# Moving the limit of the row-wise units and the time of eight early output projections in a fused attention and MLP kernel

## The chip, the cores and the metric

One core of one Trainium2 chip runs the whole program. The metric is the device time of one execution in microseconds (us). A single run differs from the next by 0.1 to 0.3%, so medians of several runs are compared, and where less than one per cent matters, both kernels run in turn on the same chip. The "span" of a run, from its first to its last instruction, is 1.7 to 2.3 us shorter than its time.

## The reference, cut to what matters

```python
# x: 2048 tokens x 512; 32 query heads, 8 KV heads, 2048 keys of 128 each
mod = silu(c) @ w_mod                       # six rows: sa, ca, ga, sb, cb, gb
h = layernorm(x) * (1 + ca) + sa
q = h @ wq
p = softmax(q k^T / sqrt(128));  o = p v    # the loop of 128 units
x = x + ga * (o @ wo)                       # the "output projections" of the units
h = layernorm(x) * (1 + cb) + sb            # second norm
z = gelu(h @ w_in); z1, z2 = halves of z    # z2 and z1 stages
g = w_sp @ layernorm(z2) + b_sp             # the "spatial product"
x = x + gb * ((z1 * g) @ w_out)
```

## The kernel before

A unit is one KV group (4 heads) with one tile of 128 queries. There are 128 units, and the main loop does one per iteration, in eight slots. "By columns" the scores come out with keys on the partitions, and PV is 64 small matmuls in the next iteration. "By rows" they come out with queries on the partitions; the rows are normalised by DVE (the vector engine) and turned by a transposing DMA, and PV is 16 wide matmuls three iterations later. An output projection, four matmuls, follows PV by two or three iterations.

```python
NU = HKV * NT                                   # 128;  CT = 4, NSLOT = 8
TURN_A, TURN_B = 2 * CT, NU - CT - 2            # 8, 122

def by_rows(u):  return TURN_A <= u < TURN_B and u % 2 == 0
def pv_at(u):    return u + 3 if by_rows(u) else u + 1
def wo_at(u):    return pv_at(u) + (3 if TURN_A <= u < TURN_B else 2)
# ... qk(u, i), rows branch: two matmuls, then
            nc.scalar.activation(out=rows_of(u, hh)[...], in_=s_ps[:], func=ACT.Exp,
                                 scale=inv_sqrt_dh, accum_out=rsums[u][:, i : i + 1])   # L1012
            if half == 1:
                at(*divmod(u * NSLOT + i + 2, NSLOT), lambda: turn_rows(u, hh))
# ... pv(u, i), by columns, after its last slot
            nc.sync.dma_start_transpose(out=oTs[u][:], in_=onorms[u]...)                # L1100
# ... wo_proj(u): four matmuls oT x wo (L1112); for the last group also residual and statistics
# ... ln2(it, j), the second norm of tile j
        def second():
            # ...
            normalise(xn[:], x_sb[:, j, :], ...)                                        # L686
            st["xnT"] = res.tile([P, NDT, P], BF16, name="xnT2", bufs=2)                # two buffers
            nc.sync.dma_start_transpose(out=st["xnT"][:], in_=xn[:])                    # L1149
        def third():
            # four tensor_scalar: hT <- xnT * (1 + cb) + sb                             # L1156
        at(it + 1, 0, first); at(it + 1, 4, second); at(it + 2, 5, third)
# ... loads
    at(2, 5, lambda: nc.gpsimd.dma_start(out=wmod_b, in_=wmod_dram[...]))               # 2 MB
    at(NU - CT - 1, 2, lambda: nc.gpsimd.dma_start(out=win_sb, in_=win_dram))
    at(4, 4, mod_cols_b)                        # first use of wmod_b: L855
    at(5, 4, mod_rows)
    # from iteration NU + 1 on: transposed loads of w_sp from SP                        # L1188
# ... main loop
    for it in range(NU + 6):
        pvs = [u for u in (it - 5, it - 3, it - 1) if 0 <= u < NU and pv_at(u) == it]
        wos = [u for u in range(max(it - 6, 0), min(it - 2, NU)) if wo_at(u) == it]
        wf = [fn for u in wos for fn in wo_proj(u)]
        for i in range(NSLOT):
            for fn in later.pop((it, i), []): fn()
            if it < NU: qk(it, i)
            # PV of pvs, this slot's part; then the fills (q projections)
            if i >= NSLOT - len(wf): wf[i - NSLOT + len(wf)]()
            if it >= NU: zrun(3)                # z2 and z1 matmuls
        # ... ln2(it, tile) for the units of the last group in wos
```

## Time and profile before

| | before |
|---|---|
| time of three runs, us | 1314.62, 1315.22, 1316.67; median 1315.22 |
| profiled run: time, span, granted clock | 1314.0, 1311.9, 1.0 |
| iteration 8, the first with scores by rows, starts at | 83.16 |
| iteration 120 starts at | 1056.22 |
| first z2, first z1, first spatial matmul | 1128.79, 1152.72, 1182.94 |
| first MLP output projection (L1458) | 1210.57 |

The table holds start times of TensorE from the timeline of its instructions; they cut the span into stretches that can be compared between kernels. In a timeline line the columns are start, duration of the group, engine, source line, operation, output<-inputs, shapes, count, and in brackets the idle time ahead of it with what ended it. Matmuls overlap, so the price of a group is the distance to the next start, not its duration. The lines themselves stand in the prediction below.

### The profile page before, as it was taken

The numbers are of one execution on the slowest core, as the hardware profiler recorded it, in microseconds if no ns is written. First come the engines' busy times: TensorE is split into PE (matmuls) and PEld (weight loads), VectorE is DVE, ScalarE is ACT, GpSimd is POOL, SyncE is SP. The second block draws the span as 40 slices with busy tenths as digits, with TensorE's granted clock in tenths as the row PEclk, the third lists the DMA queues.
The fourth block names the chain that finished last, engine by engine and source line by source line (L and its number), as shares of the span: only waits on it lengthen the run. The fifth ranks groups of instructions, "written<-read, shape, count | busy, mean of one in ns | idle before, by whom it ended". The sixth has DMA issues, their size and how long they took to land.

```text
span 1311.9 us, 24470 instructions
## 1 busy us (share of the span) xinstructions
PE 1304.1 (99%) x9623; PEld 741.0 (56%) x9623; DVE 682.6 (52%) x1675; ACT 1111.1 (85%) x1517; POOL 54.0 (4%) x96
## 2 busy tenths in 40 slices
PE   9999999999999999999999999999999999999998
PEld 5665555555555555555555555555555556644445
DVE  5644544444445454444545444444454577884444
ACT  7899999999999999999999999999999998650000
POOL 1200000000000000000000000000000011120000
PEclk9999999999999999999999999999999999999999
DMA  7589778977787797779986798678866673254300
GB/s 181 119 118 178 130 140 147 148 130 149 153 156 142 140 140 142 142 139 136 160 162 121 144 142 156 124 150 153 153 125 128 116 131 85 58 138 100 73 20 27
DMA packets 592170, 170.51 MB, mean 130 GB/s; under 512 B 581712, under 2 KB 588112, under 8 KB 592048
## 3 DMA queue, kind: packets, MB, share of 16 engines
q1 hardware_dynamic: 585024, 149.74, 64.5%
q0 software_dynamic: 4432, 16.91, 5.1%
q10 hardware_dynamic: 2592, 2.23, 0.5%
q8 instruction: 77, 1.26, 0.4%
q14 instruction: 45, 0.37, 0.1%
HBM read 21.89 MB, written 2.10 MB: 18 GB/s over the span
## 4 chain that ended last, share of the span: by engine, by line
PE 98%; DMA 1%; DVE 0%; ACT 0%; SPq 0%; issue 0%; DVEq 0%
PE o_ps L1080 19%; PE s_ps L1024 18%; PE s_ps L1005 15%; PE o_ps L1059 15%; PE misc L1112 8%; PE misc L945 8%; PE misc L1437 7%; PE s_ps L1271 2%; PE s_ps L1310 2%; PE o_ps L1458 1%; DMA oT<-onorm 1%; PE o_ps L786 1%; PE s_ps L1458 1%; PE misc L855 0%; PE o_ps L945 0%; DVE hT L814 0%
## 5 line engine op out<-in xcount | busy, mean ns | idle before, releaser
L1031 ACT ACTIVATE pT<-s_ps 128x1024 bf16<-128x1024 f32 x560 | 568.5, 1024 | 34.4 <-PE s_ps L1024 11.3
L1080 PEld LDWEIGHTS <-pT 128*128 128x128 bf16 x4480 | 299.6, 98 | 130.8
L1080 PE MATMUL o_ps<-v,pT 128*128 128x129 bf16 x4480 | 344.6, 220 | 0.0
L1024 PE MATMUL s_ps<-qT,kT 128*128 128x512 bf16 x1136 | 337.6, 379 | 0.3 <-ACT pT L1031 0.2
L1005 PE MATMUL s_ps<-kT,qT 128*128 128x512 bf16 x912 | 271.2, 379 | 0.0
L1012 ACT ACTIVATE win_sb<-s_ps 128x1024 bf16<-128x1024 f32 x228 | 233.3, 1024 | 3.4
L1112 PE MATMUL misc<-wo_g,oT 128*128 128x512 bf16 x512 | 194.1, 379 | 0.7 <-DMA oT<-onorm 0.7
L945 PE MATMUL misc<-hT,wq_g 128*128 128x512 bf16 (+2 forms) x520 | 187.0, 371 | 0.1
L1024 PEld LDWEIGHTS <-kT 128*128 128x128 bf16 x1136 | 110.2, 98 | 114.6 <-issue 2.4
L1012 ACT ACTIVATE pn<-s_ps 128x1024 bf16<-128x1024 f32 x152 | 155.4, 1023 | 2.0 <-ACT wmod_a L1012 0.3
L1059 PEld LDWEIGHTS <-v 128*128 128x128 bf16 x912 | 89.2, 98 | 107.7
L956 DVE CAST qT<-misc 128x512 bf16<-128x512 f32 x125 | 85.6, 684 | 123.1 <-PE misc L945 123.1
L1068 DVE CAST oT<-o_ps 128x512 bf16<-128x512 f32 x57 | 39.4, 691 | 192.3 <-PE o_ps L1059 192.3
L1059 PE MATMUL o_ps<-wsp,v 128*128 128x512 bf16 x464 | 137.3, 379 | 0.0
L1059 PE MATMUL o_ps<-pT,v 128*128 128x512 bf16 x448 | 133.2, 379 | 0.0
L1005 PEld LDWEIGHTS <-qT 128*128 128x128 bf16 x912 | 89.1, 98 | 59.8 <-issue 0.2
L1045 DVE TENSOR_TENSOR tot<-rs 128x1 f32<-128x1 f32 x228 | 35.0, 153 | 127.7 <-ACT win_sb L1012 85.3
L1437 PE MATMUL misc<-wsp,z 128*128 128x512 bf16 (+2 forms) x560 | 100.7, 336 | 0.0
L1050 DVE TENSOR_SCALAR win_sb<-win_sb,rall 128x2048 bf16<-128x2048 bf16 x114 | 85.9, 753 | 4.2 <-DVE rall L1048 0.3
L1437 PEld LDWEIGHTS <-z 128*128 128x128 bf16 x560 | 50.6, 98 | 48.5
L1012 ACT ACTIVATE wmod_a<-s_ps 128x1024 bf16<-128x1024 f32 x76 | 77.8, 1024 | 0.0
L1125 DVE TENSOR_TENSOR xacc<-misc,xacc 128x512 f32<-128x512 f32 x112 | 76.1, 679 | 0.0
(110 smaller groups left out, 831.0 us busy)
## 6 DMA issues: line engine op xcount, KB each, us to landing
wq_g<-in_A_wq_dram POOLq DMA_DIRECT2D x7, 512.0 KB, 6.1
v<-in_A_v_cache_dram POOLq DMA_DIRECT2D x7, 512.0 KB, 6.3
wo_g<-in_A_wo_dram POOLq DMA_DIRECT2D x7, 512.0 KB, 10.6
wsp<-in_w_mod_dram POOLq DMA_DIRECT2D x1, 2048.0 KB, 10.8
out_dram<-yout ACTq DMA_DIRECT2D x16, 128.0 KB, 1.7
win_sb<-in_B_w_in_dram POOLq DMA_DIRECT2D x1, 1792.0 KB, 7.9
x_sb<-in_A_x_dram SPq DMA_DIRECT2D x3, 512.0 KB, 5.9
oT<-onorm SPq DMA_TRANSPOSE x71, 2.8
```

Of the source, the lines that this page charges most:

```text
L945: nc.tensor.matmul(ps[0][:, o0 : o0 + n], lhsT=wqs[g][:, dt, hh * DH : (hh + 1) * DH], rhs=hTs[ch][:, dt, c0 : c0 + n], start=(dt == 0), s ...
L956: nc.vector.tensor_copy(out=dst, in_=src)
L1005: nc.tensor.matmul(s_ps[:, c * 512 : (c + 1) * 512], lhsT=qTs[b][:, hh, jj * P : (jj + 1) * P], rhs=groups[g]["kT"][:, k0 : k0 + 512], sta ...
L1012: nc.scalar.activation(out=rows_of(u, hh)[:, half * HK : (half + 1) * HK], in_=s_ps[:], func=ACT.Exp, scale=inv_sqrt_dh, accum_out=rsums[u ...
L1024: nc.tensor.matmul(s_ps[:, h * 512 : (h + 1) * 512].rearrange("p (r q) -> p r q", r=REP), lhsT=groups[g]["kT"][:, kt * P : (kt + 1) * P], ...
L1031: nc.scalar.activation(out=pTs[u][:, 2 * i : 2 * i + 2, :], in_=s_ps[:].rearrange("p (k q) -> p k q", k=2), func=ACT.Exp, scale=inv_sqrt_dh,)
L1050: nc.vector.tensor_scalar(out=rows, in0=rows, scalar1=rinv, scalar2=None, op0=ALU.mult)
L1059: nc.tensor.matmul(o_pss[u][:], lhsT=groups[g]["v1"][:, kt, 0:DH], rhs=pTs[u][:, kt, :], start=(kt == 0), stop=(kt == NKT - 1),)
L1080: nc.tensor.matmul(o_ps[:, hh % 2, 0 : DH + 1], lhsT=pTs[u][:, kt, hh * P : (hh + 1) * P], rhs=groups[g]["v1"][:, kt, 0 : DH + 1], start=( ...
L1112: nc.tensor.matmul(X_ps[:], lhsT=oTs[u][:, hh, :], rhs=groups[g]["wo"][:, hh, :], start=(hh == 0), stop=(hh == REP - 1),)
L1125: nc.vector.tensor_tensor(out=xaccs[j][:], in0=X_ps[:], in1=xaccs[j][:], op=ALU.add)
L1437: nc.tensor.matmul(g_ps[:, :n], lhsT=z2[:, st, f * P : (f + 1) * P], rhs=wsp[t][:, st, c0 : c0 + n], start=(st == 0), stop=(st == NT - 1 a ...
```

## The change

The intent has two parts. **Part one** turns units 122 and 124 from columns to rows, and so the load of `win_sb`, which overwrites row buffers, has to be issued later. **Part two** puts the output projections of units 0 to 7 three iterations behind PV instead of two, as the later units have it. The last units, which come after unit 121, are two iterations behind.

```diff
-    TURN_A, TURN_B = 2 * CT, NU - CT - 2
+    TURN_A, TURN_B = 2 * CT, NU - 2
@@
-        return pv_at(u) + (3 if TURN_A <= u < TURN_B else 2)
+        return pv_at(u) + (3 if u < TURN_B - CT else 2)
@@
-    at(NU - CT - 1, 2, lambda: nc.gpsimd.dma_start(out=win_sb, in_=win_dram))
+    at(NU - 2, 4, lambda: nc.gpsimd.dma_start(out=win_sb, in_=win_dram))
```

## The prediction

> **What bounds the kernel now.** The page first: share of busy time per engine, then the slices.
>
> ```profile
> PE 1304.1 (99%) x9623; PEld 741.0 (56%) x9623; DVE 682.6 (52%) x1675; ACT 1111.1 (85%) x1517; POOL 54.0 (4%) x96
> ```
>
> TensorE is busy 99% of 1311.9 us. That count may hide pipelining, so I read its spacing in the timeline of its instructions. The attention loop runs one unit (four heads of 128 queries against 2048 keys) per iteration, in eight slots. A unit is done either "by columns" (scores QK at L1024, PV at L1080: 64 small matmuls) or "by rows" (QK at L1005, PV at L1059: 16 wide ones, after a transposing DMA, three iterations later). One slot of each kind, from the regular part of the loop:
>
> ```profile
> 1056.22 0.59 PE L1005 MATMUL s_ps<-kT,qT 128*128 128x512 bf16 x2
> 1056.65 0.62 PE L1080 MATMUL o_ps<-v,pT 128*128 128x129 bf16 x8
> 1057.11 0.38 PE L945 MATMUL misc<-hT,wq_g 128*128 128x512 bf16 x1
> 1057.32 0.59 PE L1005 MATMUL s_ps<-kT,qT 128*128 128x512 bf16 x2
> ...
> 1065.03 0.59 PE L1024 MATMUL s_ps<-qT,kT 128*128 128x512 bf16 x2
> 1065.46 0.59 PE L1059 MATMUL o_ps<-pT,v 128*128 128x512 bf16 x2
> 1065.89 0.38 PE L945 MATMUL misc<-hT,wq_g 128*128 128x512 bf16 x1
> 1066.11 0.59 PE L1024 MATMUL s_ps<-qT,kT 128*128 128x512 bf16 x2
> ```
>
> The starts tell the price: two wide matmuls take 0.43 us (1065.46 to 1065.89), so **0.216 us** each; eight small ones take 0.455 us (1056.65 to 1057.11), so **0.057 us** each. A slot is 1.10 us with PV by columns, 1.08 by rows. No waits stand between them: here TensorE is the bound, at full clock (PEclk is 9 in every slice).
>
> ScalarE is the second limit. The timeline of its instructions gives one exp per 0.915 us where nothing holds it (1095.42: eight in 7.86 less start-up), but about 1.10 by rows, because a read of the accumulator follows each:
>
> ```profile
> 1056.86 1.02 ACT L1012 ACTIVATE win_sb<-s_ps 128x1024 bf16<-128x1024 f32 x1
> 1057.78 0.19 ACT L1012 ACTIVATION_READ_ACCUMULATOR win_sb<-s_ps 128x1 f32 x1
> 1057.95 1.02 ACT L1012 ACTIVATE win_sb<-s_ps 128x1024 bf16<-128x1024 f32 x1
> ```
>
> Where a unit's QK is by rows and a slot has no fill (no q projection L945, no output projection L1112), TensorE could do 0.43 + 0.455 = 0.885 us but is held at 1.00, as iteration 10 shows:
>
> ```profile
> 100.34 0.59 PE L1005 MATMUL s_ps<-kT,qT 128*128 128x512 bf16 x2
> 100.77 0.61 PE L1080 MATMUL o_ps<-v,pT 128*128 128x129 bf16 x8
> 101.34 0.59 PE L1005 MATMUL s_ps<-kT,qT 128*128 128x512 bf16 x2
> ```
>
> Last, the list of waits. The only sizable one of TensorE on another engine in the loop is this, and the chain of waits shows its source:
>
> ```profile
> 79.63 0.39 PE L1112 MATMUL misc<-wo_g,oT 128*128 128x512 bf16 x1 [0.72 <-DMA oT<-onorm]
> ```
>
> ```profile
> 66.82 12.77 DMA oT<-onorm
> ```
>
> **What the Trainium skill says.** "TensorE: Matmul & The Clock Gate", Back-to-back issue gap: the gap of an isolated warm matmul is N/2.4 + 2.5 ns, that is 216 ns at 512 columns and 56 at 129, but in streams of weight loads and matmuls about 131 and (at 128) 81. This trace has 0.216 and 0.057 although every matmul here has its own weight load, so it agrees with the isolated formula, not the stream figures. This matters: at 81 ns a unit by columns would cost 64 x 0.081 = 5.2 us and the change would gain over 1.5 us per unit. "Perfetto Trace Analysis", Identifying the Most-Contended Engine: matmul busy share does not tell how near the roofline TensorE is. Agreed; hence the spacing above. "DMA: Bandwidth & Descriptors", Issuing engines are not separate DMA queues: DMAs from all engines share the 16 DMA engines and interleave. The trace agrees: the oT transpose above took 12.8 us (median 2.8) behind four hT transposes, with three loads of 512 KB from GpSimd in flight.
>
> **Part one: units 122 and 124 by rows.** Only even units from 8 up to the limit are by rows, so moving the limit from 122 to 126 turns two units.
> TensorE: 64 x 0.057 = 3.62 us becomes 16 x 0.216 = 3.45: 0.17 per unit, **-0.35** in all.
> ScalarE: 8 accumulator reads per unit, exp 0.915 to 1.10 per slot: +1.5 us per unit. DVE: 4 x (0.153 + 0.164 + 0.753) + 0.691 = 4.97 us takes the place of 2 x (0.169 + 0.424) = 1.19, +3.8 per unit.
> Which of it lies on the path depends on the iteration, so I re-laid 122 to 127, each from an iteration of like content:
> - 122: QK by rows; 8.81 before, 8.81 after (as 120).
> - 123: PV of two units before, 12.26; one after, 8.63 (as 121): -3.63.
> - 124: QK by rows with four slots that have no fill, ScalarE holds TensorE; 8.00 to 8.21 (like iteration 8): +0.21.
> - 125: PV by rows, one output projection instead of two, four slots at the exp pace 0.915; 8.81 to 7.92: -0.89.
> - 126: 8.80 both.
> - 127: two PVs now (124, 126) and no q projection: 12.26 - 4 x 0.216 = 11.40 against 8.00: +3.40.
> - 129: one output projection more (unit 124's): +0.86.
> Sum **-0.05**: the 0.35 saved is spent on about 0.3 of waiting for exp.
>
> The load of win_sb must follow the last row unit, since it overwrites row buffers. It took 7.9 us when issued at 1087. Issued at iteration 126, slot 4, near 1111 to 1116, it lands by 1124, and its first use is near 1127.4: hidden, unless delayed by 3 us or more.
>
> **Part two: output projections of units 0 to 7 one iteration later.** No instruction is added. Unit 4's projection moves from iteration 7 to 8, so the wait goes: the matmul before it ended its issue at 78.75, the start is 79.63: **-0.88**. Iteration 3 loses four matmuls: -0.86, less about 0.05 because ScalarE then limits. Iteration 11 gains them, but it runs at the exp pace (0.915 per slot where TensorE needs 0.865), so it grows only from 7.27 to 4 x 0.90 + 4 x 1.08 = 7.92: +0.68 with rounding. Sum **-1.1**; I take **-1.0**.
>
> **DVE at the end.** Both projections moved late (122's to 127, 124's to 129) bring in the last group about 2.95 us of DVE work each (residual, statistics) and 1.4 of normalising. The windows by iteration show DVE full there; the last two below are iterations 129 and 130:
>
> ```profile
> 1128.34:1136.80 8.46, 8.46 (x90) 6.07 (x89) 6.23 (x19) 3.67 (x4) 0.79 (x2) 1.00 0.29 58
> 1136.80:1142.20 5.40, 5.40 (x29) 2.74 (x28) 4.23 (x11) 2.75 (x3) 0.79 (x2) 1.00 0.36 58
> 1142.20:1147.60 5.40, 5.40 (x29) 2.74 (x28) 5.23 (x13) 2.75 (x3) 0.47 (x2) 1.00 0.48 105
> ```
>
> (third number after the span: DVE busy). About 3.4 us more before the first z1 activation, 1.2 of it left after DVE's gaps and the longer iteration 129. That activation already waits for DVE:
>
> ```profile
> 1154.77 1.02 ACT L1318 ACTIVATE z1T<-s_ps 128x1024 bf16<-128x1024 f32 x1 [0.94 <-DVE stz L1293]
> ```
>
> TensorE needs its bank back at about 1156.2, 0.4 after this one ends, so up to 0.85 us could be lost. My reading of this dependency is unsure; I count half, **+0.4**. Later the queue of DVE work has 1.95 us idle at 1160 and about 3.5 of slack before the spatial product needs the last z2.
>
> Total: -0.05 - 1.0 + 0.4 = -0.6: 1315.2 becomes **1314.6 us**.
>
> **Rivals.** (a) *The end gets worse*: win_sb late or DVE late. For it: DVE is over 90% busy in iterations 118 to 120, and the load's lead shrinks from 41 us to some 12 to 16. Against: the shares of DMA time are only 0.08 to 0.28 in 125 to 127. It would cost 1 to 4 us: 1316 to 1319. (b) *PV by columns is dearer than its spacing shows*, as the skill's 81 ns would have it: gain 3 us more, 1311 to 1312. Against: the spacing is read from thousands of matmuls here, and the bound slots agree. (c) *The early wait only moves*: the projections of units 4 to 7 now meet the first row units' transposes in the queue. Each has a whole iteration (8 to 9 us) more, against transposes of 4.5 us; then part two gives nothing and the time stays at 1315 to 1315.6.
>
> **Range and chances.** The three runs before span 1314.6 to 1316.7, so +-1 us is noise of a median. With rival (a) on one side and (b) on the other, 1312.4 to 1316.6 should hold it 8 times in 10. Two per cent is 26 us; no part here is a tenth of that, so "within 2%" is nearly certain.
>
> **What would show it.** No wait on oT near 79 us, and a longer iteration 11; PV of unit 122 in sixteen matmuls of 0.216 us; iteration 123 near 8.6 and 127 near 11.4 us; exp holding TensorE in 124; win_sb landed before the first z2 matmul; the first z1 activation 1 to 2 us later. The prediction is wrong if the first z2 matmul waits for win_sb, if DVE holds the z1 stage by more than 2 us, or if a row transpose is late for PV in 125 or 127.

## The result, and the profile after

| | before | after |
|---|---|---|
| median of 4 runs, us | 1314.92 (1313.66 to 1316.67) | 1313.61 (1312.94 to 1314.2) |
| span of the profiled run | 1311.9 | 1312.3 |
| ratio, 95% interval | | 0.9989 (0.9972 to 1.0006) |

A ratio is the mean time of one kernel's runs over that of the other's runs of the same rounds, so it is not quite the ratio of the medians. The medians say -1.3 us, but the spans of the two profiled runs say +0.4 (their times +0.2). Neither can be read alone at this size; the stretches tell what happened inside the span.

| start of, us | before | after | difference |
|---|---|---|---|
| iteration 1 | 18.46 | 18.39 | -0.07 |
| iteration 4 | 45.41 | 44.48 | -0.93 |
| products with w_mod (L855) | 48.98 | 48.94 | -0.04 |
| iteration 8 | 83.16 | 82.23 | -0.93 |
| iteration 12 | 115.02 | 114.74 | -0.28 |
| iteration 120 | 1056.22 | 1055.95 | -0.27 |
| first z2 matmul | 1128.79 | 1127.61 | -1.18 |
| first z1 matmul | 1152.72 | 1152.39 | -0.33 |
| first spatial matmul | 1182.94 | 1182.62 | -0.32 |
| first MLP output projection | 1210.57 | 1211.01 | +0.44 |

The busy line of the page after, under the heading of busy time per engine. Some matmul records are missing (9355 matmuls, 9527 weight loads), so starts are used and not counts.

```profile
PE 1294.0 (99%) x9355; PEld 736.5 (56%) x9527; DVE 689.3 (53%) x1693; ACT 1113.0 (85%) x1533; POOL 55.7 (4%) x96
```

DVE and ScalarE gained work (682.6 to 689.3 us and 1111.1 to 1113.0), as part one says, and TensorE stays the bound.

The timeline of the matmuls at the two places where part two acts, after: the products with w_mod in iteration 4, then, in a fence of its own, the projection that waited at 79.63 before.

```profile
48.94 0.95 PE L855 MATMUL misc<-sc_bf,wsp 128*128 128x1 bf16 x32 [0.70 <-DMA wsp<-in_w_mod_dram]
```

```profile
78.72 0.38 PE L1112 MATMUL misc<-wo_g,oT 128*128 128x512 bf16 x1
```

And the first of these before:

```profile
48.98 0.94 PE L855 MATMUL misc<-sc_bf,wsp 128*128 128x1 bf16 x32
```

The wait on oT is gone, and 0.9 us with it. But iteration 3, shorter by 0.86, brought TensorE to the w_mod products earlier than their 2 MB load, and 0.70 of it went into a wait that was not there before.

The end of the loop after, in the timeline of TensorE: unit 124's scores at L1005 instead of L1024 (iteration 124), and its PV as wide matmuls in iteration 127.

```profile
1092.63 0.59 PE L1005 MATMUL s_ps<-kT,qT 128*128 128x512 bf16 x2
...
1117.05 0.59 PE L1024 MATMUL s_ps<-qT,kT 128*128 128x512 bf16 x2
1117.48 1.03 PE L1059 MATMUL o_ps<-wsp,v 128*128 128x512 bf16 x4
1118.35 0.59 PE L1024 MATMUL s_ps<-qT,kT 128*128 128x512 bf16 x2
```

Four wide matmuls take 0.87 us from start to start, 0.217 each. Iterations 122 to 127 last 8.81, 8.63, 8.21, 7.91, 8.81 and 11.39 us, which is the prediction's 8.81, 8.63, 8.21, 7.92, 8.80 and 11.40. From iteration 120 to the first z1 matmul the kernel before takes 96.50 us and the one after 96.44.

What came later than that was not foreseen. DVE's timeline, before: the last tile of the second norm (L1156), and the first small operation after the last z2 normalisation (L1409).

```profile
1162.07 0.98 DVE L1156 TENSOR_SCALAR hT<-xnT,modc 128x128 bf16<-128x128 bf16 x4 [1.95 <-DMA xnT<-xn]
...
1182.67 0.42 DVE L1409 TENSOR_SCALAR tmp<-rall 128x512 f32<-128x512 f32 x1
```

The same two after:

```profile
1165.87 0.98 DVE L1156 TENSOR_SCALAR hT<-xnT,modc 128x128 bf16<-128x128 bf16 x4 [3.85 <-DMA xnT<-xn]
...
1186.47 0.42 DVE L1409 TENSOR_SCALAR tmp<-rall 128x512 f32<-128x512 f32 x1
```

DVE waits 1.90 us longer for the transpose and finishes z2 3.80 us later. The spatial product, which starts within 0.32 us of the same time in both, needs that z2 at its sixteenth matmul. Its group in TensorE's timeline, before and then after; the second number is the length from the first start to the last end.

```profile
1182.94 27.79 PE L1437 MATMUL misc<-wsp,z 128*128 128x512 bf16 x128
```

```profile
1182.62 28.55 PE L1437 MATMUL misc<-wsp,z 128*128 128x512 bf16 x126
```

It became 0.76 us longer. Why was the transpose of xn late? First the queue of DMA issues from SP (the engine that issues all transposes), after; then what ended SP's wait ahead of L1149 (total, times, longest), from the list of waits between 1157 and 1161; then DVE's timeline:

```profile
1153.06 5.38 SPq L1188 DMA_TRANSPOSE wsp<-in_B_w_sp_dram  x4
1159.85 1.21 SPq L1149 DMA_TRANSPOSE xnT<-xn  x1
```

```profile
SPq L1149 <- DVE hT L1156: 2.2, 1, 2.2
```

```profile
1158.89 1.82 DVE L1156 TENSOR_SCALAR hT<-xnT,modc 128x128 bf16<-128x128 bf16 x8
```

The xn of the last tile was ready at 1157.67 (start 1157.26 and 0.41 of work), but its transpose was issued only at 1159.85 and landed by 1165.87. SP had w_sp transposes ahead of it, but these were issued by 1158.44. What ended the wait was DVE's modulation of an earlier tile: there are two xnT buffers, and the last transpose needs one of them back. Part one puts the output projections of units 124 and 126 into one iteration, 129, so that their two tiles take both buffers together (their transposes are issued in one group, at 1150.49) and are modulated together, the eight operations above. The fourth of these, the last that reads the first buffer, ends at 1159.82, and the issue follows 0.03 us later. Before, the buffer had been free since 1150.7; xn was ready at 1156.66 and its transpose was issued at 1156.69. So of the 3.80 us of later landing, 1.01 comes from DVE's added work ahead of xn, 2.15 from the wait to issue, which the buffer ended, and 0.64 from the time between issue and DVE's start (6.02 us instead of 5.38). That the buffer is the cause is read from these times and from the same label in e1, e3, e4, e5, r_after and r_both; in e8_rows_third_later the w_sp issues took longer and ended last. A third buffer was not tried.

### The profile page after: what moved, and what is told of

Same layout as the page of the kernel before. It is cut to its first block, busy times and chain, and to the rows that moved or that the text cites. A ratio compares the mean times of both kernels' runs of the same rounds, so it can differ in the third digit from the quotient of the medians. Undisturbed runs are those within 1.5% of the kernel's fastest.

```text
span 1312.3 us, 24168 instructions
## 1 busy us (share of the span) xinstructions
PE 1294.0 (99%) x9355; PEld 736.5 (56%) x9527; DVE 689.3 (53%) x1693; ACT 1113.0 (85%) x1533; POOL 55.7 (4%) x96
## 4 chain that ended last, share of the span: by engine, by line
PE 96%; DMA 1%; issue 1%; DVE 1%; ACT 0%; SPq 0%; POOL 0%; DVEq 0%; ACTq 0%
PE o_ps L1080 19%; PE s_ps L1024 18%; PE s_ps L1005 16%; PE o_ps L1059 15%; PE misc L1112 8%; PE misc L945 8%; PE misc L1437 7%; PE s_ps L1271 2%; PE s_ps L1310 2%; PE o_ps L1458 1%; DMA wsp<-in_w_mod_dram 1%; PE s_ps L1458 0%; DMA kT<-in_A_k_cache_dram 0%; DVE hT L814 0%; DMA hT<-xn 0%
## 5 line engine op out<-in xcount | busy, mean ns | idle before, releaser
L1031 ACT ACTIVATE pT<-s_ps 128x1024 bf16<-128x1024 f32 x552 | 561.1, 1025 | 31.5 <-PE s_ps L1024 9.5
L1080 PEld LDWEIGHTS <-pT 128*128 128x128 bf16 x4416 | 295.3, 98 | 128.9
L1080 PE MATMUL o_ps<-v,pT 128*128 128x129 bf16 x4416 | 339.7, 220 | 1.5
L1024 PE MATMUL s_ps<-qT,kT 128*128 128x512 bf16 x1104 | 328.1, 379 | 1.4 <-ACT pT L1031 0.2
L1005 PE MATMUL s_ps<-kT,qT 128*128 128x512 bf16 x917 | 274.9, 379 | 3.0
L1012 ACT ACTIVATE win_sb<-s_ps 128x1024 bf16<-128x1024 f32 x238 | 243.7, 1025 | 3.5
L1112 PE MATMUL misc<-wo_g,oT 128*128 128x512 bf16 x468 | 177.4, 379 | 0.6
L945 PE MATMUL misc<-hT,wq_g 128*128 128x512 bf16 (+2 forms) x482 | 173.3, 370 | 0.8
L1024 PEld LDWEIGHTS <-kT 128*128 128x128 bf16 x1104 | 107.2, 98 | 115.0 <-issue 2.3
L1012 ACT ACTIVATE pn<-s_ps 128x1024 bf16<-128x1024 f32 x156 | 159.6, 1025 | 2.0 <-ACT wmod_a L1012 0.3
L956 DVE CAST qT<-misc 128x512 bf16<-128x512 f32 x125 | 85.7, 685 | 122.9 <-PE misc L945 122.8
L1005 PEld LDWEIGHTS <-qT 128*128 128x128 bf16 x944 | 92.2, 98 | 61.6
L1050 DVE TENSOR_SCALAR win_sb<-win_sb,rall 128x2048 bf16<-128x2048 bf16 x119 | 89.6, 753 | 4.4 <-DVE rall L1048 0.3
L1012 ACT ACTIVATE wmod_a<-s_ps 128x1024 bf16<-128x1024 f32 x78 | 79.9, 1024 | 0.0
```

The costliest lines, as they stand in the source:

```text
L945: nc.tensor.matmul(ps[0][:, o0 : o0 + n], lhsT=wqs[g][:, dt, hh * DH : (hh + 1) * DH], rhs=hTs[ch][:, dt, c0 : c0 + n], start=(dt == 0), s ...
L956: nc.vector.tensor_copy(out=dst, in_=src)
L1005: nc.tensor.matmul(s_ps[:, c * 512 : (c + 1) * 512], lhsT=qTs[b][:, hh, jj * P : (jj + 1) * P], rhs=groups[g]["kT"][:, k0 : k0 + 512], sta ...
L1012: nc.scalar.activation(out=rows_of(u, hh)[:, half * HK : (half + 1) * HK], in_=s_ps[:], func=ACT.Exp, scale=inv_sqrt_dh, accum_out=rsums[u ...
L1024: nc.tensor.matmul(s_ps[:, h * 512 : (h + 1) * 512].rearrange("p (r q) -> p r q", r=REP), lhsT=groups[g]["kT"][:, kt * P : (kt + 1) * P], ...
L1031: nc.scalar.activation(out=pTs[u][:, 2 * i : 2 * i + 2, :], in_=s_ps[:].rearrange("p (k q) -> p k q", k=2), func=ACT.Exp, scale=inv_sqrt_dh,)
```

## The experiments

Four things were open: what each part is worth by itself, where the z2 delay comes from, whether the price per row unit holds, and why the kernel before scatters more than the one after. In four calls, each had eleven runs of the kernel before on the same chip: medians 1315.25, 1317.11, 1316.95 and 1315.1 us. Because those medians move with the kernel's own scatter, I give each experiment's own median, the span of its profiled run, and the stretches.

### e1_rows_only: part one alone

The kernel after, with the projections of units 0 to 7 back at two iterations.

```diff
-        return pv_at(u) + (3 if u < TURN_B - CT else 2)
+        return pv_at(u) + (3 if TURN_A <= u < TURN_B - CT else 2)
```

> Part one alone: units 122 and 124 by rows, projections of units 0 to 7 as before. Theory (from the two traces): TensorE reaches the first z1 matmul about 0.06 us earlier than in the kernel before (-0.92 in iterations 122 to 127, +0.86 in 129), and then loses about 0.8 us in the first spatial product, because DVE finishes the last z2 normalisation some 3.8 us later. So about +0.7 us against before in a profile, the wait on oT near 79 us still there. Rival: the rows pay 0.35 us as the TensorE sum says and the tail costs nothing; then -0.1 to -0.4 us and no wait in the spatial product.

Measured: median 1316.79 us, 1313.9 to 1322.58; ratio 1.0019 (0.9999 to 1.0039); span 1312.1. The span is only 0.2 us above that of the kernel before, and not the expected 0.7, because the wait on oT was 0.28 us here instead of 0.89 (iteration 7 lasts 9.09 us instead of 9.70, and 8.81 without a wait). Iteration 120 to the first z1 matmul takes 96.45 us against 96.50, so part one saves the predicted 0.05 there. The spatial stretch takes 28.56 us against 27.63, a wait on z2 of 0.93. So the end loss belongs to part one. Three of the six runs were above 1317, and none of the runs of the kernel after had been: the first sign that part two does something to the scatter.

### e2_wo_only: part two alone

The kernel before, with the rule for all units below the limit.

```diff
-        return pv_at(u) + (3 if TURN_A <= u < TURN_B else 2)
+        return pv_at(u) + (3 if u < TURN_B else 2)
```

> Part two alone: output projections of units 0 to 7 one iteration later, rows as before. Theory: -0.86 us in iteration 3 is given back at iteration 4, where the first matmul with the second part of w_mod waits for its load; -0.9 us at iteration 7 where the wait on oT goes; +0.7 us at iteration 11. So -0.2 to -0.3 us at iteration 12 against before, and no wait in the spatial product. Rival (the prediction's sum): -1.0 us, nothing given back to a load.

Measured: median 1313.35 us, 1312.64 to 1313.98; ratio 0.9981 (0.9967 to 0.9995); span 1311.4. The spatial stretch is 27.62, without the wait. Iteration 8 starts at 81.39, 1.77 us before that of the kernel before: the sum of the prediction's -0.88 and -0.86. The expectation that the w_mod products always give the 0.86 back fell. The load is issued at about the same time (37.1 against 37.65) but landed at 46.9 here and 48.9 in the kernel after. It is a race between TensorE and a load, won or lost from run to run.

### e3_cols_later: no wait for w_mod

The kernel after, with the w_mod products two slots later.

```diff
-    at(4, 4, mod_cols_b)
+    at(4, 6, mod_cols_b)
```

> The changed kernel with the w_mod column products (32 tiny matmuls) two slots later in iteration 4, after the load has landed. Theory: the wait on that load (0.70 us idle, 0.86 with what it hid) goes and iteration 12 starts 0.8 us earlier than in the changed kernel; the spatial product's wait on DVE grows by as much as TensorE comes earlier, so the end moves by only 0 to -0.3 us. Rival: the two waits are independent and the end moves by -0.8 us.

Measured: median 1313.81 us, 1313.26 to 1314.71; ratio 0.9986 (0.9972 to 1.0); span 1312.0. Iteration 8 starts at 81.40 instead of 82.23, so the edit does its work early. Its spatial product in TensorE's timeline:

```profile
1184.96 25.83 PE L1437 MATMUL misc<-wsp,z 128*128 128x512 bf16 x114 [0.42 <-DVE z L686]
```

The product starts at 1181.78, 0.84 us earlier than after, and then waits (the line is the part after the wait), so that the stretch from its start to the first output projection is 28.84 us: the wait on z2 grew to 1.21. About half of what was won early is lost to a later wait that was already there. The two waits stand in series: with the first one gone, the second grew by 0.45 us. The first output projection starts 0.39 us earlier than after, a little more than the 0 to 0.3 expected.

### e4_third_later: the modulation of the last tile leaves DVE's way

In the kernel after, DVE took its instructions in the order of the program: it stood idle for 3.85 us at the modulation that waits for xnT, with z2 statistics behind it that were ready. Here, for the last tile alone, it is queued five slots later.

```diff
-        at(it + 2, 5, third)
+        at(*((it + 2, 5) if j < NT - 1 else (it + 3, 2)), third)
```

> The changed kernel with the last unit's four DVE instructions that wait for the xnT transpose moved behind three z2 statistics in DVE's order. Theory T1 (one late transpose blocks DVE's queue): DVE's idle of 3.85 us before them shrinks to under 0.5, the last z2 normalisation ends 3 us or more earlier, the first spatial product has no wait, end -0.7 to -0.8 us against the changed kernel. Theory T2 (the sheer DVE work of the two projections moved late is what delays z2): the idle time only moves, the wait stays above 0.5 us and the end is the same.

Measured: median 1313.19 us, 1312.53 to 1316.41; ratio 0.9984 (0.9968 to 1.0); span 1311.8. DVE's timeline at the same two places, then TensorE's spatial group:

```profile
1166.39 0.98 DVE L1156 TENSOR_SCALAR hT<-xnT,modc 128x128 bf16<-128x128 bf16 x4 [0.44 <-DMA xnT<-xn]
...
1183.39 0.42 DVE L1409 TENSOR_SCALAR tmp<-rall 128x512 f32<-128x512 f32 x1
```

```profile
1182.78 27.79 PE L1437 MATMUL misc<-wsp,z 128*128 128x512 bf16 x126
```

The transpose is as late as after, but DVE's wait for it falls from 3.85 to 0.44 us, the z2 work ends 3.1 us earlier, and the spatial product is back at 27.79. This shows the cause of the 0.76 us: it is the late transpose that blocks DVE's queue. The rival, that the added DVE work alone overruns, falls: what remains (L1409 is 0.61 us after the spatial start here, 0.27 before it in the kernel before) is about 0.9 us, and the 3.5 us of slack hold that.

### e5_both, r_both: both edits, on two chips

The edits of e3 and e4 together in the kernel after; r_both is a repeat. It was run at another time.

> The changed kernel with both edits: w_mod column products two slots later, and the last unit's four xnT instructions later in DVE's order. Theory: two independent waits on TensorE's path, 0.86 us (w_mod load) and 0.76 us (z2 normalisation), both go: span near 1310.7 us, 1.6 below the changed kernel's profile, time about 1312.0 (2.5 to 3 under before). Rival: removing one wait exposes another load or DVE step, as the z2 wait grew to 1.21 us when only the first edit was made; then no better than either edit alone, 1313.

> The version with both edits once more, on the same chip as the changed kernel. Theory: 1.0 to 1.6 us under the changed kernel in the same rounds, and no wait of TensorE on the w_mod load or on z2. Rival: 0 within 0.5 us, the edits' gain was noise.

Measured: e5_both 1312.69 us (1312.51 to 1314.87), ratio 0.9968 (0.9951 to 0.9985), span 1311.0; r_both 1313.18 (1312.55 to 1314.69), ratio 0.9979 (0.9965 to 0.9992), span 1310.9. Neither waits for w_mod or z2; both spatial stretches are 27.63. The spans are 1.3 and 1.4 under that of the kernel after (1.6 was expected) and 0.9 and 1.0 under that of the kernel before. The ratio of e5_both looks better than it is, since the runs before in that call were the slow ones.

### r_after: the kernel after again

> The changed kernel once more, unaltered, beside the version with both edits. Theory: the two waits are there in its profile again (the w_mod one depends on when the load lands, 46.9 to 49.1 us so far, and may be absent), span 1311.5 to 1312.4, time 1313 to 1314. Rival: the waits of its first profile were chance, and the z2 wait is absent.

Measured: median 1314.0 us, 1312.96 to 1314.95; ratio 0.9984 (0.9971 to 0.9997); span 1311.1. The load of w_mod landed at 47.7 and there is no wait for it; the wait on z2 is there (spatial stretch 28.27, DVE idle 3.75 for xnT). So the z2 wait is in both profiles of this kernel, and the w_mod wait in one. The gap to r_both is 0.8 us, less than the 1.0 to 1.6 expected; in the profile one of the two waits was absent, and the other runs were not traced. All ten runs of the kernel after together have a median of 1314.0.

### e6_turn_at_48: the price of a row unit

The kernel after, with the rows beginning at unit 48: twenty units fewer by rows. The 81 ns of the rival are the figure for streams that the prediction quotes from the Trainium skill, "TensorE: Matmul & The Clock Gate", Back-to-back issue gap.

```diff
-    TURN_A, TURN_B = 2 * CT, NU - 2
+    TURN_A, TURN_B = 12 * CT, NU - 2
```

> The changed kernel with units by rows from 48 instead of 8: 20 units more by columns in the regular part of the loop, the ends untouched. Theory: a unit by columns costs TensorE 64 x 0.0566 - 16 x 0.2155 = 0.17 us more, so +3.4 us against the changed kernel (pair of iterations 17.61 us where it was 17.44). Rival: weight loads set the pace in streams (81 ns per small matmul), so +1.7 us per unit, +35 us in all; or ScalarE's and DVE's lighter work gives it all back, 0.

Measured: median 1316.37 us, 1315.96 to 1317.05; ratio 0.9994 (0.9978 to 1.001); span 1314.6. A slot of the regular part, now wholly by columns, in TensorE's timeline:

```profile
207.87 0.59 PE L1024 MATMUL s_ps<-qT,kT 128*128 128x512 bf16 x2
208.30 0.62 PE L1080 MATMUL o_ps<-v,pT 128*128 128x129 bf16 x8
208.75 0.38 PE L945 MATMUL misc<-hT,wq_g 128*128 128x512 bf16 x1
208.97 0.59 PE L1024 MATMUL s_ps<-qT,kT 128*128 128x512 bf16 x2
```

The slot is 1.10 us again, eight small matmuls 0.45. Iteration 124 starts at 1093.33, and in r_after, also without a w_mod wait, at 1089.76. That is 3.57, or 3.47 after a head start of 0.10: 0.17 us for each of 20 units, as the prediction has it. At 81 ns per small matmul it would have been some 35 us; that rival is out by a factor of ten.

### e7_wo_cols_later: part two with the w_mod edit, without part one

The kernel of e2_wo_only with the edit of e3_cols_later.

> Part two alone plus the later w_mod column products; rows end at unit 122 as before. Theory: all of part two's gain is kept (-0.86 in iteration 3, -0.9 at 7, +0.7 at 11, so -1.1 us) and the z stage has no wait: span near 1310.8, the same as with both edits and the two row units, because part one is worth only 0.06 us. Rival: the two row units are worth their 0.35 us of TensorE work, and this is slower than the kernel with both edits by 0.3 us or more.

Measured: median 1313.33 us, 1312.8 to 1314.37; ratio 0.9972 (0.9955 to 0.9988); span 1310.8. In span that equals e5_both (1311.0) and r_both (1310.9), which have part one as well: the theory holds inside the span.

In time it does not quite. e5_both has a median 0.64 us lower and a mean 0.42 lower, as the rival has it. Runs show a difference that lies outside the span: time less span is 2.08 to 2.26 us in each of 69 runs without part one (before, e2, e7, e9, e10; mean 2.16) and 1.74 to 1.93 us in each of the 52 with it (mean 1.81). So part one takes about 0.34 us off the time outside the span. e6_turn_at_48 has this too, with twenty row units fewer, so it does not go by the number of row units; what it is, no trace shows. Spans of kernels with and without part one must therefore not be compared as if they were times.

### e8_rows_third_later: part one with its end repaired, without part two

The kernel of e1_rows_only with the edit of e4_third_later.

> Part one alone with the last unit's xnT instructions later in DVE's order, so without its loss in the z stage. Theory: part one is then worth 0.06 us: span 1311.8 to 1312.0 if the wait on oT near 79 us is as long as in the kernel before (up to 0.9 less if it is shorter), from the start of iteration 120 to the end of the first spatial product 0.1 us less than in the kernel before. Rival: the 0.35 us of TensorE work is all saved: 0.3 us or more less over that stretch.

Measured: median 1315.18 us, 1313.51 to 1318.37; ratio 0.9996 (0.9981 to 1.0011); span 1311.7. The stretch from iteration 120 to the first MLP output projection holds all that part one does. It is 154.35 us before, 154.34, 154.35 and 154.35 in e2_wo_only, e7_wo_cols_later and e10_unit4_only (columns), 155.06 after, and 154.29 here and 154.30 in r_both (rows, repaired). So inside the span part one is -0.06 at best, and +0.71 in the kernel after; the 0.34 outside the span comes on top. The rival, that the whole 0.35 of TensorE work comes out over this stretch, falls: the rest is the waiting for exp that the prediction counted. In this profile there was no wait on oT at all: iteration 7 lasts 8.81 us, with unit 4's projection where it was before.

### e9_wait_long: a longer wait on purpose

The runs of the kernel before fall in two groups: 16 of 48 lie above 1317 us, with a mean of 1318.5 and a granted clock of 0.997 to 0.999, and the other 32 have a mean of 1315.0. No profile had caught a long one. A guess was that the wait on oT at 79.6 us is longer in those runs, long enough for the clock to fall. Here the kernel before asks for that projection at the start of iteration 7, four slots early, so that the wait must be long.

```diff
+        w0 = 0 if it == TURN_A - 1 else NSLOT - len(wf)
@@
-            if i >= NSLOT - len(wf):
-                wf[i - NSLOT + len(wf)]()
+            if w0 <= i < w0 + len(wf):
+                wf[i - w0]()
```

> The kernel before with unit 4's output projection four slots earlier in iteration 7, so that TensorE's wait on the oT transpose grows from 0.9 to about 5 us. Question: why do the kernels without part two show runs of 1317 to 1322.6 us at a granted clock of 0.996 to 0.998, and the kernels with part two none? Theory C: in those runs a wait at an early output projection is some us long, and TensorE's clock is granted only in part for a few us after it. Then here most runs lose more than the 4.3 us of added wait: 1321 to 1324 at a clock of 0.996 to 0.998. Rival: the wait costs its own length only, 1319 at a clock of 0.999, and the long runs are something else.

Measured: median 1322.13 us, 1321.82 to 1323.19; ratio 1.0049 (1.0036 to 1.0061); span 1319.7; clock 0.996 to 0.997 in all six runs. TensorE's timeline around the wait:

```profile
80.55 0.61 PE L1112 MATMUL misc<-wo_g,oT 128*128 128x512 bf16 x1 [5.50 <-DMA oT<-onorm]
80.95 1.06 PE L1024 MATMUL s_ps<-qT,kT 128*128 128x512 bf16 x2
81.80 1.07 PE L1080 MATMUL o_ps<-v,pT 128*128 128x129 bf16 x8
...
85.90 0.59 PE L1024 MATMUL s_ps<-qT,kT 128*128 128x512 bf16 x2
```

The windows of the same stretch. After the window and its length come the busy times of PE, PEld, DVE, ACT and POOL; the third number from the end is the granted clock.

```profile
75.00:80.00 5.00, 0.05 (x1) 0.00 (x0) 0.00 (x0) 0.50 (x1) 1.31 (x2) 0.89 1.25 40
82.00:84.00 2.00, 2.00 (x13) 1.16 (x11) 0.00 (x0) 1.02 (x1) 0.00 (x0) 0.50 0.03 5
86.00:88.00 2.00, 2.00 (x22) 1.29 (x20) 0.98 (x3) 1.18 (x2) 0.00 (x0) 1.00 0.00 0
```

After a wait of 5.50 us TensorE works at half its clock: two wide matmuls take 0.85 us from start to start instead of 0.43, until 85.7. The loss is 4.6 of waiting (5.50 less the 0.88 of before) and about 2.6 of half-rate work (5.1 us at half rate), 7.2 of the 7.8 us between the spans. The Trainium skill, "TensorE: Matmul & The Clock Gate", Part 1: The HAM clock gate, says that the array falls to half rate after an idle window of about 3.4 us and comes back after about as long of sustained work. This trace agrees with the fall: TensorE stood idle from 75.05, and the mean clock of 0.89 from 75 to 80 puts the fall near 78.9, some 3.8 us in (an estimate from that mean). The way back took longer here, 5.1 us of work at 0.50. A wait of 0.9 us in the kernel before did not bring the clock down.

This shows that a longer wait at this place costs more than its length and lowers the mean clock of a run to about what the long runs have. It does not show that the long runs are made in this way, for none of them was traced.

### e10_unit4_only: one projection moved

The kernel before, with unit 4 alone at three iterations, the unit whose oT was waited for.

```diff
-        return pv_at(u) + (3 if TURN_A <= u < TURN_B else 2)
+        return pv_at(u) + (3 if u == 4 or TURN_A <= u < TURN_B else 2)
```

> The kernel before with the output projection of unit 4 alone one iteration later. Theory: unit 4's wait on oT is the whole of what part two removes: its wait of up to 0.9 us in the profile goes, and the runs above 1317 us go too (13 of 37 in the kernel before): six runs within 1313 to 1315.5 at a clock of 0.999. Rival: other units of 0 to 7 have the long waits; then one or more of six runs lies above 1317 at a clock below 0.999.

Measured: median 1312.83 us, 1312.53 to 1314.12; ratio 0.9978 (0.9966 to 0.9991); span 1310.4, the shortest of all; no run above 1317. Iteration 12 starts at 113.42, 1.60 us earlier than before, of which 0.44 was already there at iteration 4, ahead of anything that was moved. The other 1.16 is the edit: iteration 7 loses the wait (0.89) and four matmuls (0.86), and iteration 8 takes these for 0.60, since two of the four slots without a fill were held by exp (0.89, 0.91, 1.01 and 1.00 us before, 1.10 each with the matmul). Of the 1.16, the 0.89 is what this one profile of the kernel before had of the wait; e1 and e8 had 0.28 and none. If one run in three is long without the edit, six clean runs have a chance of 9%, so the six runs alone are not proof.

With its runs, the kernels in which unit 4's projection is one iteration later (after, r_after, r_both, e2 to e5, e7, e10) have 52 runs and none above 1317, the highest being 1316.41. The two with unit 4 as before and the rows turned (e1, e8) have 4 of 12. (e6_turn_at_48, which is longer by construction, and e9_wait_long are left out.)

| version | median, us | span | runs above 1317 |
|---|---|---|---|
| before (48 runs) | 1314.9 to 1317.1 by call | 1311.9 | 16 |
| after (10 runs in all) | 1314.0 | 1312.3, 1311.1 | 0 |
| part one alone (e1_rows_only) | 1316.79 | 1312.1 | 3 of 6 |
| part two alone (e2_wo_only) | 1313.35 | 1311.4 | 0 of 6 |
| both parts and both edits (r_both) | 1313.18 | 1310.9 | 0 of 6 |
| unit 4's projection alone (e10_unit4_only) | 1312.83 | 1310.4 | 0 of 6 |

The last has the shortest profiled span and is the smallest change. It beats both kernels in span and median; from e5_both and r_both the runs do not separate it, and e5_both has the lowest median (1312.69).

## Why the prediction was right, and where it was not

The time (1314.6 against 1313.61, and 1314.0 over ten runs), the range and "within 2%" held. That says little by itself: the interval of the ratio runs from -3.7 to +0.8 us, wider than the predicted change of -0.6. The terms are checked one by one.

- **Part one, -0.05.** Right inside the span, and to the step: each iteration length within 0.01 us, and -0.05 to -0.06 in the stretch up to z1 in every kernel with rows there. e8_rows_third_later shows it up to the MLP. The 0.34 us outside the span was not foreseen.
- **The price, 0.17 us per unit.** Right; e6_turn_at_48 measured it on twenty units.
- **Part two, -1.0.** Each term is there: the wait (-0.88), iteration 3 (-0.86), iteration 11 (+0.65 against a predicted +0.68). What failed is the sum, for two reasons. It leaves out that an earlier TensorE meets the load of w_mod: in the profiles where that load was late (landing at 48.9 and 49.05, after and e4_third_later) iteration 4 lasts 9.67 and 9.73 us instead of 8.80, so about 0.9 us was given back; in e2_wo_only, r_after and e6_turn_at_48 nothing was. And it takes the wait of one profile for that of every run, while e1_rows_only and e8_rows_third_later had 0.28 and none. Against that one profile the term is between -0.2 (after) and -1.1 (e2_wo_only).
- **Sums and readings.** "Sum **-1.1**" does not follow from its terms, which give -1.01; the -1.0 taken is right. "About 1.10 by rows" for exp is TensorE's pace in that slot: in iteration 10, where exp holds TensorE, exps start at 100.19, 101.18, 102.18 and 103.17, so the accumulator read costs 0.08 us per slot and not 0.185, or 0.6 us per unit instead of "+1.5". This did no harm, because the lengths were taken from like iterations. The eight exps at 1095.42 were not at full pace either; iteration 11 has eight in 7.44 us, which gives the 0.915. "DVE full there" is true of the third window alone (5.23 of 5.40 us; the others are 74% and 78%). And of the three loads "in flight" at 66.82, that of wq_g had landed at 64.2.
- **"I count half, +0.4" for the z1 activation.** Wrong: from the first z1 matmul to the first spatial matmul it is 30.22 us before and 30.23 after, so the cost there is 0. The activation came 2.05 us after its first matmul before and 2.06 after. Its line after, from ScalarE's timeline, names DVE again with the same idle time, but for another piece of DVE's work:

```profile
1154.45 1.02 ACT L1318 ACTIVATE z1T<-s_ps 128x1024 bf16<-128x1024 f32 x1 [0.94 <-DVE bnst L697]
```

  The activation kept its distance to its own eight matmuls (8 x 0.216 = 1.73, and their end) while DVE's work changed, so I read it as waiting for those, and DVE's label as a second event close by. No run took the two apart.
- **"1.95 us idle ... and about 3.5 of slack".** This is the step that failed. The 3.5 us was right (1182.67 against the need at 1182.94 + 15 x 0.216 = 1186.18). But the 1.95 of idle was taken as room for added work, and it was a wait for a transpose that the added work makes later. It grew to 3.85, because the added tile also held the buffer that the last transpose needed, and the loss was 0.76 us. e4_third_later shows that this wait is the cause by taking it out of DVE's way. By chance the 0.76 lost here stands near the 0.4 counted at the wrong place, so that the total came out close.
- **Rival (a), the end gets worse.** Right in kind, small in size, and by DVE, not by `win_sb`: that load was issued at 1111.9 and no z2 matmul waited for it at 1127.6.
- **Rival (b)** fell to e6_turn_at_48. **Rival (c)** fell: iteration 8 of e2_wo_only starts 1.77 us earlier.
- **Not foreseen at all:** the scatter. The three runs before ended at 1316.67, and the prediction took that for noise of a median. A third of the runs before are some 3.5 us longer, and the kernels with the projection moved have none of these. Part two is therefore worth up to about 1.1 us in the profiled runs, and the long runs besides. That the long wait and the halved clock make the long runs is argued, from e9_wait_long and the counts. It is not shown.

## What to carry to other kernels

Price a conversion from one form of matmul to another by start-to-start spacing, and lay out every iteration that it touches with the engine that will limit there; part one's 0.35 us of saved TensorE work came out as 0.05 in the span. Idle time ahead of an instruction is not slack if what ends it moves with the change: ask what issues the transfer that ends it, what stands ahead of it in that queue, and who must first give back the buffer that it writes; on DVE, a waiting instruction could be put behind ready ones (e4_third_later). Compare times as well as spans. Look at the spread of many runs, not at one profile, before judging a wait that varies: a wait of 0.9 us in the one profile was absent in another, and with its removal went the third of runs that were 3.5 us longer.

## What the Trainium skill lacked or had wrong

- "TensorE: Matmul & The Clock Gate", Back-to-back issue gap: the stream figures of about 81 ns (128 columns) and 131 ns (512) do not hold here. With one weight load per matmul the starts are 57 ns apart at 129 columns and 216 ns at 512, which the page's isolated formula gives; twenty units changed from one form to the other differ by 3.47 us, 0.17 per unit.
- "ScalarE: Activation LUTs", What it computes: it names the accumulator output but no cost. In these traces it is an instruction of 0.19 us after each exp; it overlaps its neighbours, and where ScalarE sets the pace the exps start 0.995 us apart instead of 0.915 at 1024 elements.
- "DMA: Bandwidth & Descriptors", Issuing engines are not separate DMA queues: it calls the time to initiate a DMA usually small relative to the DMA itself. For transposes from SP it was not: 1.21 us to issue xnT, out of a median 2.5 us from issue to landing, and 5.38 us to issue four w_sp transposes.
- No page gives how much the landing of one and the same load varies from run to run: the 2 MB load of w_mod took 9.2 to 12.0 us over the profiles, and with it a wait of 0.7 us came and went.
